# A three-layer chain on one core: the first layer's front by seven products instead of eight, and all attention ahead of it

## The chip, the cores and the metric

The kernel runs on one core of a Trainium2 chip. Its engines run side by side, each through its own instructions in order: TensorE (PE; its weight loads are listed as PEld), VectorE (DVE), ScalarE (ACT), GpSimd (POOL) and SyncE (SP), whose queue issues most DMA transfers. The metric is the device time of one launch in microseconds (us).

## The reference

Three stages follow one another on 2304 tokens (4 batches of 576) of 512 features:

```python
scores = scale * np.matmul(q, k.transpose(0, 1, 3, 2))   # 8 heads of 64
ret = scores * Dmat                                       # causal decay gamma_h ** (i - j)
x = np.matmul(ret, v)                                     # tokens x 512
# layer A, d_ff 1536
xn = x / np.sqrt(np.mean(x * x, -1, keepdims=True) + 1e-06) * rms_g
g = xn @ w_gate
x2 = (g * (1.0 / (1.0 + np.exp(-g))) * (xn @ w_val)) @ w_out
# layer B, d_ff 2048
h = x2 @ w_in
out = np.where(h >= 1, h, np.where(h <= -1, 0.0, (h + 1) ** 2 / 4)) @ w_out2
```

The weights arrive as 64-bit floats, in pairs of 32-bit words.

## The kernel before, in words

**Threefold products.** The products run in the type fp32r. Each fp32 operand is split into a high part rounded to it and the low rest (`split`: a cast on ScalarE, a subtraction on VectorE), and each product is issued three times (`three`): high by high, low by high, high by low, into one PSUM bank.

**Attention** goes by chunks of 128 tokens (the fifth of a batch has 64). `scores` multiplies K and Q of the 8 heads; VectorE applies the decay table; GpSimd scales Q and K (`qs`, `ks`). `values` adds what the batch's running state gives (`state`), the chunk's own part, and the chunk's addition to the state, which VectorE adds in SBUF. ScalarE copies the result out of PSUM and squares it; GpSimd sums the squares over features (`sq`, `sum`). Batches come one after the other. The first 7 chunks run ahead of layer A, the other 13 between its products (`att_step` in `step_a`).

**Layer A** takes the tokens in five blocks of 512, 512, 384, 512 and 384, and for each the 12 slices of 128 hidden features: 60 steps. A step has two front products (gate and value), each of 4 x 3 matmuls, then sigmoid on ScalarE and two multiplications and a split on VectorE, and 4 x 3 matmuls back for the previous step's slice, summed over the 12 slices in four banks. In the first block each step's weights are converted from 64-bit words (`convert`: Prelu on ScalarE, shift and merge on VectorE), stored as fp32 in DRAM (`wa32`), and split; later blocks load them back and split them again.

**Layer B** takes blocks of 768 tokens. Its front is already done by Strassen's algorithm in Winograd's form: token halves and feature halves make a 2 x 2 product out of 7 products (`product`) instead of 8, of sums of the weights (`prepare_in`) and of x (`sums_x`). Its weights are converted, summed and split while layer A runs (`prepare`, in the steps that `PREPARE` lists), stored in DRAM split, and loaded for each of the 24 steps. The back products of a step fill the gaps between the front products of the next.

**Order.** Nothing is issued as it is written. Class `Plan` records every operation (so the trace gives one line, L135, for all), and `issue` sorts them by a list schedule with a cost per operation and due times counted backward from TensorE's order. It keeps each engine's own queue in the order it finds; TensorE's rank is the program's order, with matmuls that are ready taken ahead by up to 100 ns.

## Time and profile before

| | before |
|---|---|
| three runs | 919.15, 920.0, 921.18 us; median 920.0 |
| profiled execution | span 920.9 us, 0.9 over the median, inside the three runs' spread |
| TensorE busy | 904.3 us (98%), 5098 matmuls |
| VectorE, ScalarE, GpSimd busy | 576.2, 482.3, 70.3 us |
| mean granted TensorE clock | 0.998 of full speed |
| DMA | 209.94 MB, mean 228 GB/s |

In the profile's rows a group is named by engine, operation, what it writes <- what it reads, with the tile names of the program, partitions x elements, and its count. `fr` are the two PSUM banks of the front products, `acc` and `at` the banks behind; `xall` holds the split x, `wt` the split weights, `h` the split hidden values; `att` are the attention buffers, used again in layer B for temporaries. Of an fp32 (not fp32r) matmul the trace shows two instructions. "Idle before" is the engine's idle time ahead of the group, with what ended it.

### The profile page before, as it was taken

What the parts mean: (1) busy time and instruction counts of PE and PEld (TensorE: products, weight loads), DVE (VectorE), ACT (ScalarE), POOL (GpSimd) and SP (SyncE); (2) the same over time, 40 slices, a digit from 0 to 9 for tenths busy, and PEclk for the clock granted to TensorE, in tenths of its full rate; (3) what the DMA queues carried; (4) which work ended last, traced back from release to release, by engine and by line L of the source; (5) the groups of instructions that cost most, each with busy time, mean ns of one, the idle gap of its engine ahead of it and who ended that gap; (6) DMA issues with size and microseconds to landing.
All of it is one profiled execution on the core that took longest, in us unless ns stands there. A gap on an engine that the chain in (4) does not pass through costs nothing.

```text
span 920.9 us, 13342 instructions
## 1 busy us (share of the span) xinstructions
PE 904.3 (98%) x5098; PEld 797.7 (87%) x5098; DVE 576.2 (63%) x929; ACT 482.3 (52%) x858; POOL 70.3 (8%) x80
## 2 busy tenths in 40 slices
PE   8799999999999999999999999999999999999998
PEld 7578888888889998888899998989888998989896
DVE  3978888888988888855658645434734345434343
ACT  3446665555765576533545454445654455644443
POOL 4620001310014001100000000000000000000000
PEclk9999999999999999999999999999999999999999
DMA  9679976988769984642254386646765454755432
GB/s 364 229 261 314 308 278 235 331 331 325 283 240 378 387 291 150 234 150 94 103 202 153 104 329 243 216 160 216 251 222 194 169 191 170 266 165 213 159 137 69
DMA packets 51647, 209.94 MB, mean 228 GB/s; under 512 B 5632, under 2 KB 11392, under 8 KB 47488
## 3 DMA queue, kind: packets, MB, share of 16 engines
q1 hardware_dynamic: 45392, 199.51, 61.2%
q10 hardware_dynamic: 6192, 9.59, 2.8%
q8 instruction: 40, 0.66, 0.3%
q14 instruction: 23, 0.19, 0.1%
HBM read 167.14 MB, written 41.94 MB: 227 GB/s over the span
## 4 chain that ended last, share of the span: by engine, by line
PE 92%; DVE 4%; DMA 2%; ACT 2%; issue 1%; ACTq 0%
PE fr L135 50%; PE acc L135 31%; PE at L135 11%; DMA out_dram<-o 1%; DMA att<-in_att_dram 1%; DVE xraw L135 1%; DVE xall L135 0%; DVE t L135 0%; DMA gk_sb<-in_gk_dram 0%; DVE w L135 0%; DVE wt L135 0%; ACT att L135 0%; DVE state L135 0%; DVE wsum L135 0%; DVE wpair L135 0%
## 5 line engine op out<-in xcount | busy, mean ns | idle before, releaser
L135 PE MATMUL fr<-xall,wt 128*128 128x384 f32 (+1 forms) x2424 | 512.1, 356 | 3.6 <-DVE xall L135 1.3
L135 PEld LDWEIGHTS fr<-xall,wt 128*128 128x128 f32 x2424 | 436.8, 188 | 53.5 <-DVE xall L135 2.4
L135 PE MATMUL acc<-h,wt 128*128 128x512 f32 (+1 forms) x708 | 158.1, 370 | 0.1
L135 PE MATMUL acc<-wprep,h 128*128 128x512 f32 x576 | 155.7, 394 | 0.5 <-ACT h L135 0.5
L135 PEld LDWEIGHTS acc<-h,wt 128*128 128x128 f32 x708 | 128.4, 188 | 18.2 <-ACT o L135 0.6
L135 DVE TENSOR_TENSOR wt<-w,wt 128x512 fp32r<-128x512 f32 (+1 forms) x118 | 114.4, 985 | 17.7 <-ACT wt L135 17.3
L135 PEld LDWEIGHTS acc<-wprep,h 128*128 128x128 f32 x576 | 106.6, 188 | 15.8 <-ACT h L135 0.9
L135 ACT CAST wt<-w 128x512 fp32r<-128x512 f32 (+1 forms) x118 | 96.7, 835 | 42.1 <-PE acc L135 23.6
L135 DVE TENSOR_TENSOR t<-fr,t 128x512 f32<-128x512 f32 (+1 forms) x120 | 76.3, 636 | 58.0 <-PE fr L135 29.5
L135 ACT ACTIVATE att<-att 128x384 f32<-128x384 f32 x156 | 79.2, 523 | 30.1 <-DVE att L135 18.2
L135 ACT CAST h<-t 128x512 fp32r<-128x512 f32 (+1 forms) x60 | 34.6, 577 | 79.3 <-DVE t L135 79.3
L135 DVE TENSOR_TENSOR att<-fr,att 128x384 f32<-128x384 f32 x48 | 26.6, 555 | 70.6 <-ACT att L135 69.6
L135 PE MATMUL at<-wprep,h 128*128 128x512 f32 x288 | 70.3, 392 | 0.0
L135 DVE TENSOR_TENSOR h<-att,h 128x384 fp32r<-128x384 f32 x96 | 52.8, 554 | 23.7 <-ACT h L135 23.1
L135 ACT ACTIVATE t<-fr 128x512 f32<-128x512 f32 (+1 forms) x60 | 33.3, 554 | 59.0 <-PE fr L135 58.7
L135 PEld LDWEIGHTS at<-wprep,h 128*128 128x128 f32 x288 | 53.7, 188 | 10.4
L135 ACT COPY att<-fr 128x384 f32<-128x384 f32 x48 | 23.0, 479 | 75.7 <-PE fr L135 70.2
L135 ACT CAST h<-att 128x384 fp32r<-128x384 f32 x96 | 48.7, 512 | 21.2 <-DVE att L135 20.0
L135 DVE SCALAR_TENSOR_TENSOR att<-att,att 128x384 f32<-128x384 f32 x48 | 26.8, 558 | 42.3 <-ACT att L135 42.3
L135 DVE TENSOR_TENSOR h<-t,h 128x512 fp32r<-128x512 f32 (+1 forms) x60 | 38.0, 634 | 14.2 <-ACT h L135 13.9
L135 DVE SCALAR_TENSOR_TENSOR att<-att,fr 128x384 f32<-128x384 f32 x24 | 13.3, 553 | 36.8 <-ACT att L135 36.8
L135 DVE TENSOR_TENSOR xall<-xraw,xall 128x512 fp32r<-128x512 f32 (+2 forms) x32 | 25.9, 828 | 2.8 <-ACT xall L135 2.4
(144 smaller groups left out, 672.5 us busy)
## 6 DMA issues: line engine op xcount, KB each, us to landing
w<-wa SPq DMA_DIRECT2D x48, 768.0 KB, 4.5
wprep<-wod SPq DMA_DIRECT2D x48, 512.0 KB, 4.0
wt<-wfd SPq DMA_DIRECT2D x24, 1024.0 KB, 5.2
wt<-wfd SPq DMA_DIRECT2D x24, 768.0 KB, 4.5
...
```

The lines of the kernel that those rows point to most:

```text
L135: call = lambda: getattr(real, method)(*args, **kwargs)
```

## The change

Layer A's front is also done by the seven products, over three blocks of 768 tokens: 36 steps, in each of which the 2 x 2 product gives gate and value of 128 hidden features for both token halves. The product back is split in 512 and 256 columns, four banks and two half-used ones; its 8 pieces fill the gaps between the front products. In the first block each step's weights are converted, summed and split (`prepare_a`) for the step after, and stored in DRAM in the split form (`store_a`: 1.8 MB, and the out weights as fp32, 0.26 MB); later blocks load them (`load_a`) and split only the out weights. `wts` are two buffers.

All attention stands ahead of A. Two batches alternate chunk by chunk; the state sums up in PSUM and ScalarE copies it out. The x of blocks two and three goes through two halves of `xout` to DRAM (`x1d`) on SP and comes back a block later. The gate uses ScalarE's Silu in the place of sigmoid and a product. Of layer B's 8 weight slices 5 are prepared in the later blocks of A, three (`LATE`) in B's first block. `later_than` lets the plan place some operations only behind a given one. Layer B's products are as before.

The order shows it at three places. First TensorE in layer A: before, a step of 12 gate and 12 value matmuls, the 12 of the previous step back, and the scores of a chunk in between (`at_0_145<-att`):

```order
L135 MATMUL fr_138<-xall_113,wt_151 128x512 x12
L135 MATMUL fr_139<-xall_113,wt_151 128x512 x12
L135 MATMUL acc_0_142<-h_154,wt_152 128x512 x3
L135 MATMUL acc_0_143<-h_154,wt_152 128x512 x3
L135 MATMUL acc_0_140<-h_154,wt_152 128x512 x3
L135 MATMUL acc_0_141<-h_154,wt_152 128x512 x3
L135 MATMUL fr_138<-xall_113,wt_152 128x512
L135 MATMUL at_0_145<-att_126 128x128 x3
L135 MATMUL fr_138<-xall_113,wt_152 128x512 x11
```

After, a whole step, 42 matmuls of 384 columns in `fr`, with pieces of 256 (`at`) and 512 (`acc`) of the previous step's slice between them (the last piece and two front products follow):

```order
L136 MATMUL fr_99<-xall,wt_64 128x384 x6
L136 MATMUL fr_100<-xall,wt_64 128x384 x6
L136 MATMUL fr_99<-xall,wt_64 128x384 x6
L136 MATMUL at_93<-h_67,wo 128x256 x6
L136 MATMUL fr_100<-xall,wt_64 128x384 x6
L136 MATMUL at_94<-h_67,wo 128x256 x6
L136 MATMUL fr_99<-xall,wt_64 128x384 x6
L136 MATMUL acc_95<-h_67,wo 128x512 x3
L136 MATMUL acc_96<-h_67,wo 128x512 x3
L136 MATMUL acc_97<-h_67,wo 128x512 x3
L136 MATMUL fr_99<-xall,wt_64 128x384
L136 MATMUL fr_100<-xall,wt_64 128x384 x6
```

The scores are gone from the steps, and the fill stands by pieces in between. Where A begins, the last chunks' values (state, then the chunk's own part) and the first front products mix on TensorE:

```order
L136 MATMUL at_93<-prep,state 128x128 x4
L136 MATMUL at_93<-prep,att_84 64x128 x8
L136 MATMUL acc_98<-att_83 64x64 x4
L136 MATMUL fr_99<-xall,wt_64 128x384 x3
L136 MATMUL at_94<-prep,state 128x128 x4
L136 MATMUL at_94<-prep,att_86 64x128 x8
L136 MATMUL fr_99<-xall,wt_64 128x384 x3
L136 MATMUL fr_100<-xall,wt_64 128x384 x4
L136 MATMUL at_93<-prep,state 128x64 x4
```

Ahead of these rows stand all the other chunks; before, 13 of 20 came later. Last, VectorE in the first block. Before, a step's gate (`t`, `h`) and the work on a next step's weights (`w`, `wt`):

```order
L135 TENSOR_TENSOR t_0_129<-fr_138,t_0_129 128x512
L135 TENSOR_TENSOR wt_151<-w_149,wt_151 128x512
L135 TENSOR_TENSOR t_0_131<-fr_139,t_0_129 128x512
L135 SCALAR_TENSOR_TENSOR w_150<-wpair_115,w_150 128x512
L135 TENSOR_TENSOR h_153<-t_0_131,h_153 128x512
L135 TENSOR_SCALAR w_149<-w_149 128x512
L135 SCALAR_TENSOR_TENSOR w_149<-wsum_116,w_149 128x512
L135 TENSOR_TENSOR wt_152<-w_150,wt_152 128x512
L135 TENSOR_SCALAR w_149<-w_149 128x512 x2
L135 SCALAR_TENSOR_TENSOR w_149<-stage_121,w_149 128x512
L135 TENSOR_TENSOR t_1_130<-fr_138,t_1_130 128x512
```

After, part of a step; the gate's seven operations (`att`, `h`, here six of them) stand between sums (`wsum`), low parts (`wt`, `wo`), and behind these rows two shifts, two merges and more sums follow up to the next step's first add:

```order
L136 TENSOR_TENSOR att_86<-fr_100,att_86 128x384
L136 TENSOR_TENSOR wsum<-wpair,wsum 128x256
L136 TENSOR_TENSOR wt_65<-wpair,wt_65 128x2x256
L136 TENSOR_TENSOR att_83<-fr_99,att_87 128x384
L136 TENSOR_TENSOR att_84<-att_86,att_85 128x384
L136 TENSOR_TENSOR wt_65<-wsum,wt_65 128x4x256
L136 TENSOR_TENSOR wo<-w32o_73,wo 128x512
L136 TENSOR_TENSOR h_67<-att_84,h_67 128x384
L136 TENSOR_TENSOR att_87<-fr_99,att_88 128x384
L136 TENSOR_TENSOR h_67<-att_83,h_67 128x384
L136 TENSOR_TENSOR wt_65<-wpair,wt_65 128x256
```

The adds out of PSUM (`fr`) are now three per step, one more than the products of gate and value, and low parts of seven weight operands stand between them instead of three.

The diff, cut to its core:

```diff
-BLOCKS = [512, 512, 384, 512, 384]
-STARTS = [sum(BLOCKS[:i]) for i in range(len(BLOCKS))]
...
+SB = 2 * TB
...
+W7 = 14 * 2 * P
...
-PREPARE = [(), (1, 3, 5, 7), (5, 7), (1, 3, 5, 7), (0, 1, 2, 3, 5, 6)]
+ATT = 6
+LATE = (3, 5, 7)
+EARLY = tuple(p for p in range(NPB) if p not in LATE)
...
+        if self.floor is not None and engine != "tensor":
+            before.add(self.floor)
...
-        table = {ACTF.Sigmoid: 1, ACTF.Abs_reciprocal_sqrt: 2}.get(kwargs.get("func"), 0)
+        table = {ACTF.Silu: 1, ACTF.Abs_reciprocal_sqrt: 2}.get(kwargs.get("func"), 0)
...
+    wfa = dram.tile([NA, P, W7], F32, name="wfa")
+    woa = dram.tile([NA, P, DM], F32, name="woa")
...
+    x1d = dram.tile([P, KD, NT], F32, name="x1d")
...
+        nc.vector.tensor_scalar(out=w, in0=w, scalar1=3, scalar2=None, op0=ALU.logical_shift_left)
...
+    def prepare_a(s):
+        prepare_front(wts[s % 2], None)
+        w = w32o[s % 2]
+        convert(w)
+        w = w.bitcast(F32)
+        split(w, wos[s % 4][:, :DM], wos[s % 4][:, DM:])
+
+    def prepare_back(p, ready):
+        convert(wpair_w)
+        for f, (w, r) in enumerate(zip(cut(wpair, DM), ready)):
+            split(w, r[:, :DM], r[:, DM:])
+            nc.sync.dma_start(out=wod[p, f], in_=r.bitcast(F32))
+
+    def store_a(s):
+        nc.sync.dma_start(out=wfa[s], in_=wts[s % 2].bitcast(F32))
+        nc.sync.dma_start(out=woa[s], in_=w32o[s % 2].bitcast(F32))
...
+    def load_a(s):
+        f = s % NA
+        load_front(wts[s % 2], wfa[f])
+        w = w32o[s % 2].bitcast(F32)
+        nc.sync.dma_start(out=w, in_=woa[f])
+        split(w, wos[s % 4][:, :DM], wos[s % 4][:, DM:])
...
+    chunks = [(b, c) for pair in ((0, 1), (2, 3)) for c in range(NCH) for b in pair]
...
+    staged = itertools.cycle(cut(xout[:, :2 * DM], DM))
...
+        x, new = banks[f"at{i % 2}"], banks[f"fr{b % 2}"]
...
-                nc.tensor.matmul(new[r, u], lhsT=ks[:, 2 * u + h], rhs=v[:, 2 * u + h], start=True, stop=True)
+                nc.tensor.matmul(
+                    new[r, u], lhsT=ks[:, 2 * u + h], rhs=v[:, 2 * u + h], start=c == 0 and u == 0, stop=c == NFULL - 1,
+                    skip_group_check=True,
+                )
...
-                if c:
-                    nc.vector.tensor_add(out=state[r, :, r], in0=state[r, :, r], in1=new[r])
-                else:
-                    nc.scalar.copy(out=state[r, :, r], in_=new[r])
+                nc.scalar.copy(out=st[r, :, r], in_=new[r])
...
+        sq = xout[:, 2 * DM:2 * DM + NPAIR * n].rearrange("p (u n) -> p u n", n=n)
+        edges = [g0] + [e for e in (TB, SB) if g0 < e < g0 + n] + [g0 + n]
+        for lo, hi in zip(edges, edges[1:]):
+            src = x[:, :, lo - g0:hi - g0]
+            if lo < SB:
+                nc.scalar.copy(out=x_j[lo // TB][:, :, lo % TB:lo % TB + hi - lo], in_=src)
+            else:
+                xs = next(staged)[:, :NPAIR * (hi - lo)].rearrange("p (u n) -> p u n", u=NPAIR)
+                nc.scalar.copy(out=xs, in_=src)
+                nc.sync.dma_start(out=x1d[:, :, lo:hi], in_=xs)
+        nc.scalar.activation(out=sq, in_=x[:, :, :n], func=ACTF.Square)
+        nc.gpsimd.tensor_add(out=sq[:, :2], in0=sq[:, :2], in1=sq[:, 2:])
+        nc.gpsimd.tensor_add(out=ss[:, g0:g0 + n], in0=sq[:, 0], in1=sq[:, 1])
...
-    def step_a(s):
-        _, t, f = steps[s]
-        T = BLOCKS[t]
...
-        nc.scalar.activation(out=u[:, :T], in_=g[:, :T], func=ACTF.Sigmoid)
-        nc.vector.tensor_mul(out=u[:, :T], in0=g[:, :T], in1=u[:, :T])
...
+    def back_a(s):
+
+        b, f = divmod(s, NA)
+        w, h = wos[s % 4], hs[s % 3]
+        big = [banks[f"acc{d}"] for d in range(KD)]
+        small = [banks[f"at{d // 2}"][:, d % 2 * 256:d % 2 * 256 + 256] for d in range(KD)]
+
+        def part(d, wide):
+            ps, q = (big[d], slice(0, 512)) if wide else (small[d], slice(512, SB))
+            c = slice(d * P, (d + 1) * P)
+            lo = slice(SB + q.start, SB + q.stop)
+            three(
+                ps, w[:, :DM][:, c], w[:, DM:][:, c], h[:, q], h[:, lo], f == 0 and (wide or d % 2 == 0), f == NA - 1,
+                skip_group_check=True,
+            )
+            if f == NA - 1 and (wide or d % 2):
+                o = next(o_next)
...
+    def gated(c):
+        g = temp("g", 2)
+        nc.scalar.activation(out=g, in_=c, func=ACTF.Silu)
+        return g
+
+    def keep(r, h, j):
+        split(r, h[:, j * TB:(j + 1) * TB], h[:, SB + j * TB:SB + (j + 1) * TB])
+
+    def step_a(s):
+        b, f = divmod(s, NA)
+        if s + 1 < NA:
+            with nc.later_than(marks[-4] if s == 0 else None):
+                prepare_a(s + 1)
+        units = back_a(s - 1) if s else []
+
+        def fill(n):
+            for _ in range(min(n, len(units))):
+                units.pop(0)()
+
+        after = split_x if f == NA - 1 else (lambda j: None)
+        w, h = wts[s % 2], hs[s % 3]
+        d, x = front_banks(s)
+        product(w, 0, d, True, False)
+        after(0)
+        if s < NA:
+            with nc.later_than(len(nc.ops) - 1):
+                store_a(s)
+        p1 = temp("p1", 1)
+        nc.scalar.copy(out=p1, in_=d)
+        product(w, 1, x, True, True)
+        after(1)
+        c = temp("c", 2)
+        nc.vector.tensor_add(out=c, in0=x, in1=p1)
+        g0 = gated(c)
+        product(w, 2, d, False, False)
+        after(2)
+        u2 = temp("u2", 2)
+        nc.scalar.copy(out=u2, in_=d)
+        fill(2)
+        product(w, 3, x, True, False)
+        after(3)
+        fill(2)
+        if s == 0:
+            rms(2, ("at0", "at1"))
+        product(w, 4, d, False, False)
+        after(4)
+        u3 = temp("u3", 2)
+        nc.scalar.copy(out=u3, in_=d)
+        nc.vector.tensor_add(out=u3, in0=x, in1=u3)
+        fill(2)
+        product(w, 5, x, False, True)
+        after(5)
+        nc.vector.tensor_add(out=u2, in0=x, in1=u2)
+        g1 = gated(u2)
+        r = temp("r", 2)
+        nc.vector.tensor_mul(out=r, in0=g1, in1=u3)
+        keep(r, h, 1)
+        fill(1)
+        product(w, 6, d, False, True)
+        after(6)
+        r = temp("r", 2)
+        nc.vector.tensor_mul(out=r, in0=d, in1=g0)
+        keep(r, h, 0)
+        fill(1)
+        if f == 0:
+            if b + 1 < NSB:
+                load_x(x1d, b + 1)
+                norm(b + 1)
+            else:
+                load_x(x2d, 0)
+            sums_x()
+        if s >= NA and s % 2:
+            limit[0] = len(slots)
+            with nc.later_than(len(nc.ops) - 1):
+                prepare_b()
+        if s + 2 >= NA:
+            if s + 2 < NSB * NA:
+                load_a(s + 2)
+            elif s + 2 == NSB * NA:
+                load_wf(0)
+                load_wo(0, 0)
+            else:
+                load_wf(1)
...
+        if q + 2 in LATE:
+            prepare_front(wts[q % 2], wfd[q + 2])
...
+    marks = []
+    for i in range(len(chunks) + 1):
+        if i < len(chunks):
+            scores(i, next(tags))
+        marks.append(len(nc.ops) - 1)
         if i:
...
+            values(i - 1)
+        for k in range(NSB - 1):
+            if ready[k] == i - 1:
+                rms(k, next(tags))
+                if k == 0:
+                    norm(0)
+                    sums_x(True)
+        if i == 4:
+            with nc.later_than(marks[2]):
+                prepare_a(0)
+    for s in range(NSB * NA):
         step_a(s)
```

## Rows read from the trace of the kernel before

**Rows 1.** The page's first part: busy us of each engine, share, instructions.
```profile
PE 904.3 (98%) x5098; PEld 797.7 (87%) x5098; DVE 576.2 (63%) x929; ACT 482.3 (52%) x858; POOL 70.3 (8%) x80
```

**Rows 2.** Stretches: start:end, length; PE, PEld, DVE, ACT, POOL busy (instructions); clock; DMA share, GB/s.
```profile
0.00:37.70 37.70, 29.76 (x362) 26.09 (x362) 20.37 (x35) 15.65 (x29) 19.05 (x25) 0.95 0.87 319
...
60.00:140.00 80.00, 79.97 (x367) 65.34 (x366) 69.57 (x116) 49.82 (x79) 3.65 (x5) 1.00 0.87 301
...
200.00:300.00 100.00, 99.92 (x612) 86.15 (x611) 84.20 (x136) 59.23 (x97) 12.96 (x16) 1.00 0.81 299
...
537.20:920.90 383.70, 378.43 (x1878) 338.76 (x1876) 162.78 (x292) 191.13 (x396) 0.00 (x0) 1.00 0.57 196
```

**Rows 3.** Chain of waits in order of time: start us, us, what.
```profile
54.29 3.01 PE fr L135 x12
...
100.68 5.44 PE fr L135 x24
...
473.59 4.16 PE fr L135 x24
```

**Rows 4.** TensorE in order of time, 164 to 176 us: start us, us.
```profile
174.31 1.05 PE L135 MATMUL at<-qs,state 128*128 128x128 f32 x8
```

**Rows 5.** GpSimd's groups by shape: busy us, mean ns of one, idle before.
```profile
L135 POOL TENSOR_TENSOR sq<-sq 128x256 f32<-128x256 f32 x14 | 14.0, 998 | 12.7 <-ACT sq L135 12.7
...
L135 POOL TENSOR_TENSOR qs<-att,gq_sb 128x512 f32<-128x512 f32 x8 | 11.5, 1435 | 76.5 <-PE at L135 65.5 <-issue 4.5 <-PE acc L135 3.6
...
L135 POOL TENSOR_TENSOR ks<-att,gk_sb 128x512 f32<-128x512 f32 x10 | 11.4, 1140 | 29.5 <-DMA att<-in_att_dram 25.2 <-PE at L135 4.3
...
L135 POOL TENSOR_TENSOR sum<-sq 128x128 f32<-128x128 f32 x14 | 8.3, 593 | 0.9
```

**Rows 6.** The opening in order of time, GpSimd: start us, us, what.
```profile
10.89 1.04 POOL L135 TENSOR_TENSOR ks<-att,gk_sb 128x512 f32<-128x512 f32 x1 [2.70 <-DMA att<-in_att_dram]
...
18.94 0.73 POOL L135 TENSOR_TENSOR sq<-sq 128x256 f32<-128x256 f32 x1
...
19.75 0.46 POOL L135 TENSOR_TENSOR sum<-sq 128x128 f32<-128x128 f32 x1
...
33.91 1.29 POOL L135 TENSOR_TENSOR qs<-att,gq_sb 128x512 f32<-128x512 f32 x1 [4.49 <-issue]
```

**Rows 7.** VectorE's groups by shape.
```profile
L135 DVE TENSOR_TENSOR wt<-w,wt 128x512 fp32r<-128x512 f32 x59 | 41.9, 711 | 6.7 <-ACT wt L135 6.5
...
L135 DVE TENSOR_TENSOR att<-fr,att 128x384 f32<-128x384 f32 x48 | 26.6, 555 | 70.6 <-ACT att L135 69.6 <-PE fr L135 1.0
...
L135 DVE SCALAR_TENSOR_TENSOR w<-stage,w 128x512 uint32<-128x512 uint32 x26 | 17.6, 685 | 0.1
...
L135 DVE TENSOR_SCALAR w<-w 128x512 uint32<-128x512 uint32 x36 | 16.1, 458 | 7.7 <-ACT w L135 7.3
...
L135 DVE TENSOR_TENSOR wprep<-wsum,wprep 128x1024 fp32r<-128x1024 f32 x8 | 11.1, 1393 | 0.5 <-ACT wprep L135 0.4
...
L135 DVE TENSOR_TENSOR wsum<-wpair 128x256 f32<-128x256 f32 x16 | 7.2, 468 | 0.1
...
L135 DVE SCALAR_TENSOR_TENSOR xraw<-xraw,gk_sb,y 128x384 f32<-128x384 f32 x8 | 4.9, 612 | 0.0
...
L135 DVE TENSOR_TENSOR wprep<-wpair,wprep 128x256 fp32r<-128x256 f32 x8 | 3.3, 415 | 0.0
...
L135 DVE TENSOR_TENSOR xall<-xraw,xall 128x768 fp32r<-128x768 f32 x12 | 11.5, 954 | 2.6 <-ACT xall L135 2.4
```

**Rows 8.** ScalarE's groups by shape.
```profile
L135 ACT ACT_TABLE_LOAD x11 | 14.1, 1283 | 3.7 <-issue 3.5
...
L135 ACT ACTIVATE t<-fr 128x384 f32<-128x384 f32 x24 | 11.8, 492 | 18.8 <-PE fr L135 18.6
```

**Rows 9.** DMA issues: queue, count, KB each, median us to landing.
```profile
x2d<-o ACTq DMA_DIRECT2D x12, 256.0 KB, 5.0
...
wsum<-in_tail_dram SPq DMA_DIRECT2D x1, 128.0 KB, 10.8
```

More of the change, by code (lines that the diff above doesn't have):

```diff
@@ L263, in moe_chain_kernel @@
-    stages = [stage_p.tile([P, DM, 2], U32, tag="stage", name="st") for _ in range(STAGE)]
-    more = [*stages, *(a.rearrange("p (n w) -> p n w", w=2) for a in (wpair_w, wsum_w))]
-    stage_of = [more[i % len(more)] if 9 <= i < 3 * NA - 2 else stages[i % STAGE] for i in range(len(slots))]
+    one = ctx.enter_context(tc.tile_pool(name="one", bufs=1))
+    psum = ctx.enter_context(tc.tile_pool(name="psum", bufs=1, space=PSUM))
+    dram = ctx.enter_context(tc.tile_pool(name="dram", bufs=1, space=DRAM))
@@ new lines, in moe_chain_kernel @@
+    stages = [one.tile([P, DM, 2], U32, name=f"stage{i}")[:, :, :] for i in range(STAGE)]
+    ss = sb("ss", NT)
+    o_sb = sb("o", 3 * DM)
+    gk_sb = sb("gk_sb", NFULL * H + KD)
+    eps = sb("eps", 1)
+    ones = sb("ones", P)
+    atts = [sb(f"att{i}", 8 * CH) for i in range(ATT)]
+    prep = sb("prep", 8 * DM)
+    dg = sb("dg", H * CH + NPAIR * (S - CH))
+    states = sb("state", 2 * NPAIR * P)
+    xout = sb("xout", 3 * DM)
+    banks = {n: psum.tile([P, 512], F32, name=n)[:, :] for n in ("at0", "at1", "acc0", "acc1", "acc2", "acc3", "fr0", "fr1")}
@@ new lines, in moe_chain_kernel, with split @@
+    gq_sb = dg[:, H * CH:]
+    state = [a.rearrange("p (u n) -> p u n", u=NPAIR) for a in cut(states, NPAIR * P)]
+    x_j = [a.rearrange("p (k n) -> p k n", k=KD) for a in cut(xraw, KD * TB)]
+    def split(src, hi, lo):
+        nc.scalar.copy(out=hi, in_=src)
+        nc.vector.tensor_sub(out=lo, in0=src, in1=hi.bitcast(F32))
+    slots = [wa[f, :, j * DM:(j + 1) * DM] for f in range(NA) for j in range(3)]
+    slots += [wb[p, k, j] for p in EARLY + LATE for k in range(2) for j in range(2)]
@@ L267, in load_slot @@
+    stage_t, loaded, taken, limit = {}, [0], [0], [3 * NA]
     def load_slot():
         i = loaded[0]
-        if i < len(slots):
-            st = stage_of[i]
-            assert all(st is not b for b in stage_t.values())
+        if i < limit[0]:
+            st = stages[i % STAGE]
             nc.sync.dma_start(out=st.rearrange("p a b -> p (a b)"), in_=slots[i].bitcast(U32))
@@ L359, in moe_chain_kernel @@
-    chunks = [(b, c) for b in range(B) for c in range(NCH)]
-    first, ahead = need(0), need(0) + AHEAD
-    buffers = [att_p.tile([P, 8 * CH], F32, tag="att") for _ in range(ATT)]
-    xraws = [xraw_p.tile([P, KD, 512], F32, tag="xraw", name="xraw") for _ in range(2)]
-    flat = xraws[1].rearrange("p k n -> p (k n)")
-    early = [*buffers, wpair, wsum, flat[:, :1024], flat[:, 1024:], o_sb[:, :]]
-    place = [early[i] for i in range(8)] + [early[i % 5] for i in range(8, 2 * ahead)]
-    place += [buffers[i % ATT] for i in range(2 * ahead, 2 * len(chunks))]
@@ new lines, in load_front @@
+    def load_front(w, src):
+        for a, b in ((0, 3), (3, 7)):
+            nc.sync.dma_start(out=w[:, a * 4 * P:b * 4 * P].bitcast(F32), in_=src[:, a * 4 * P:b * 4 * P])
+    def load_a(s):
[5 more added lines that the diff above has]
+    chunks = [(b, c) for pair in ((0, 1), (2, 3)) for c in range(NCH) for b in pair]
+    place = [*atts, wpair, wsum] + [atts[i % ATT] for i in range(2 * len(chunks))]
@@ L677, in product, with front_banks @@
             )
+    def front_banks(step):
+        d, x = banks["fr0"], banks["fr1"]
+        if step % 2:
+            d, x = x, d
+        return d[:, :TB], x[:, :TB]
+    def back_a(s):
[13 more added lines that the diff above has]
+                o = next(o_next)
+                nc.scalar.copy(out=o, in_=banks[f"acc{d}" if wide else f"at{d // 2}"])
+                if wide:
+                    nc.scalar.dma_start(out=x2d[:, d, b * SB:b * SB + 512], in_=o)
+                else:
+                    o = o.rearrange("p (d n) -> p d n", d=2)
+                    nc.scalar.dma_start(out=x2d[:, d - 1:d + 1, b * SB + 512:(b + 1) * SB], in_=o)
+        return [lambda d=d, wide=wide: part(d, wide) for wide in (False, True) for d in range(KD)]
```

492 lines of the change are left out of this document (148 added, 344 removed).

## The prediction

> **What bounds the kernel now.** I read the busy shares first, then the stretches, then the chain of waits, then the groups of instructions. The shares say that TensorE works 904.3 of the 920.9 us [rows 1]. By stretches, TensorE is full from 60 us on (79.97 of 80, 99.92 of 100), while VectorE is already 84 to 87% busy there; only the opening has holes: 29.76 us of work in the first 37.7 [rows 2]. The chain shows what a full TensorE costs: 24 products of 512 columns take 5.44 us and 24 of 384 take 4.16 [rows 3], so 226.7 and 173.3 ns each, 53.4 ns per 128 columns and some 13 ns besides. So a change pays here by products taken away, and loses wherever TensorE has to wait; today it waits for 16.6 us in all.
>
> **The sum by TensorE.** Layer A now: 60 steps, 36 of 512 tokens and 24 of 384; each has 24 products in front and 12 behind. That is 36 x 36 x 226.7 ns + 24 x 36 x 173.3 ns = 443.5 us. After: 36 steps (3 blocks of 768 tokens, 12 steps each) of 7 x 6 = 42 products of 384 columns (7.28 us), and behind 12 of 512 and 12 of 256. No row has a rounded-fp32 product of 256 columns. By the line through 512 and 384 it is 120 ns; the nearest row with a fresh 128 x 128 weight load each time is the state product, 8 in 1.05 us, 131 ns [rows 4]. A loss of weight-load cover could not show below 120, so I take 120 and keep +432 x 11 ns = 5 us for the upper end. A step is then 7.28 + 2.72 + 1.44 = 11.44 us, 36 are 411.9 us: TensorE loses 31.6 us of work. That is all the change has to gain; the rest is where it makes TensorE wait. I add the time by four stages.
>
> At this split a rule of the Trainium skill speaks against the change. The 384-column pair passes every 173.3 ns [rows 3], so its weight load costs at most the 13 ns that columns don't explain. The Trainium skill (TensorE: Matmul & The Clock Gate, "LDWEIGHTS" and "The mechanism") puts a 128-column load at some 107 ns and says that it overlaps running matmuls only on other row groups. By that rule the 256-column products would cost about 107 ns more each, 46 us in all; the trace contradicts it at 384 columns, and I leave it a small chance.
>
> **Stage 1, the opening: 86 us.** Now 7 of the 20 attention chunks run ahead and 13 between the products of A; the first unbroken dozen of A's products starts at 54.29 us [rows 3]. After, all 20 run ahead. TensorE isn't the slow one there: a full chunk's GpSimd work is 1.435 + 1.140 + 0.998 + 0.593 = 4.17 us at mean prices [rows 5]. All of GpSimd's work is 70.3 us [rows 1], and the change leaves it nearly as it is (two pieces fewer at block edges): 70. The last 4 us (the last chunks' sums) hold nothing up. The first of it can start at 10.89 us, when K and V of the first chunk have landed [rows 6]. Never idle, it would let A start at 10.9 + 66 = 77 us. As idle as in the opening now, where at most 19.05 us of its work lie in the 26.8 us from 10.9 to 37.7 (71%) [rows 2], it would be 104. Two things that held it then are gone: each chunk waited for its own batch's state, and now two batches alternate, and the state sums up in PSUM. I take 88% busy, 9 us of holes: 86, nearer the low end; bounds 77 and 104. VectorE's share lies beside it: 32 score multiplies of 512 and 8 of 256 (26 us by the nearest rows, 0.711 and 0.415), the first block's norm, sums and lows (14.5), two norm factors (6) and the first weights (8.4), 55 us or 64% of the stage [rows 7]; where that cover fails, A starts late within the same 104.
>
> **Stage 2, the first sweep of A: 160 us.** TensorE needs 12 x 7.28 + 11 x 4.16 = 133 us (step 0 has nothing to fill in). VectorE needs more. Preparing one step's weights is now [rows 7]: a shift of 1024 (no row; between 0.46 and 0.92, I take 0.73) and one of 512 (0.458), three merges (2.06), four sums of 256 (1.87), lows of 512, 1024 and 256 (0.711 + 1.393 + 0.415) and of the out weights (0.711): 8.35 us. The gate is 7 operations of 384 columns at 555 ns: 3.89. Together 12.2 us in a step of 11.44. Ten whole preparations fall into the sweep and 5.3 us of another; with 12 gates, the next block's norm (4 x about 1.0, from 612 ns at 384 columns), four sums and seven lows of 768 (11 x 0.954) and 2 us of the last norm this makes 152 us. Even with no hole it ends 2 us after that: 154. At the 87% of the first sweep now [rows 2] (where TensorE was the bound, so a floor) it would be 175. VectorE has weights to prepare whenever the gate doesn't call, so I take 95%: 160. The waits show as TensorE waiting for VectorE's adds out of PSUM: behind a late add stand the next products into that bank and, in TensorE's order, everything else.
>
> The DMA of this stage is 1.5 MB of raw weights, 1.8 + 0.26 MB stored per step, 3.6 MB in 13.3 us, 270 GB/s; now 301 GB/s run beside a full TensorE [rows 2], so I give it nothing. On SP's queue the stores stand in front of the raw loads of the next step; if a store is late, the loads, ScalarE's conversion and VectorE's shift are late behind it, which is the 175.
>
> **Stage 3, sweeps two and three: 279 us.** 24 x 11.44 = 274.6. VectorE falls to 3.89 + 0.71 us per step, plus a B weight every second step. Loads are 2.05 MB per step and up to 1.2 MB for B, 284 GB/s, under the 301 that hid. The shortest cover in a step is between product 4 and 5, where copy and add (under 0.5 by the row for sigmoid [rows 8], and 0.56, and their hand-overs) stand against two or three wide fills (1.4 to 2 us). I add 4 us for all of these and for the block ends, from 0 to 10.
>
> **Stage 4, layer B: 388 us.** Now 383.7 [rows 2]. The step of A left over costs 4.16 instead of 0.7 there: +3.5. Three of eight B weights are now prepared inside the first block: 6.5 us at most beside 6.1 of gate (11 operations of 555 ns) in a step of 16, VectorE 42% busy on average: 1 us, up to 5.
>
> **At no cost.** ScalarE's own Silu takes the place of sigmoid and a multiply; nearest row 492 ns for sigmoid of 384 columns [rows 8]; ScalarE is 59% busy in the sweep [rows 2], and that hides it (without cover: 72 x 0.5 us). The table loads fall from 11 to 4, 9 us [rows 8], hidden by the same slack already, so no gain.
>
> 86 + 160 + 279 + 388 = 913 us of profiled time. The profile's 920.9 is 0.9 above the median of 920.0, so the forecast is **912 us**.
>
> **Rivals.** (a) VectorE's excess in the first sweep hides behind TensorE (its holes elsewhere take it): stage 2 is 135, the total 887. For: TensorE was full at 87% VectorE. Against: only two weight buffers, so no step's preparation can start before the step two ahead has freed its buffer. (b) Slower: the staging store of the opening. 14 pieces of x go through two halves of one buffer to DRAM, on SP behind the loads of chunks, and ScalarE's third copy waits for the first store to land; behind that copy, in ScalarE's order, wait the squares and the state copies, and for them GpSimd and TensorE. A store of this size lands in 5.0 us, but a transfer of the present opening took 10.8 [rows 9]. Two chunks then need 10.8 + 1 us, 5.9 per chunk instead of 4.2: 14 x 1.7 = 24 us more, 936. It decides from about 9 us of landing on. (c) VectorE and GpSimd keep each other waiting. The undisturbed prices 1.29, 1.04, 0.73 and 0.46 [rows 6] stand against the means of [rows 5]; over the opening (12 + 16 + 16 + 16, and halves of them for the tails) they sum to 56 us. VectorE's operations with both inputs in SBUF are some 25 us there (norm 4, sums and lows 10.5, norm factors 4, first weights 7). If each holds GpSimd up in full, it works 81 instead of 70: 11 us, total 923. The Trainium skill (SBUF — State Buffer, "Who interferes with whom") states just this, an exclusive lock for the whole instruction; GpSimd's 70 us, 14 over the undisturbed sum, bear out a part of it. (d) Weight loads uncovered at 256 columns, bounded by a whole 384-column pair in place of the product: 432 x 53 ns = 23 us, 935. That the change doesn't do its sevenths is excluded by the order of TensorE's instructions.
>
> **Numbers.** Forecast 0.60, its own range 898 to 926 (stage 1 from 79 to 94, stage 2 from 154 to 168, not both ends at once); (a) 0.12; (b) 0.13; (c) 0.11; (d) 0.04. Of the forecast's case I put three quarters more than 0.2% under 920.0 (this is about what a measurement here can tell from no change), a tenth within; with (a), and a fifth of (c), this makes 0.60 faster. Same: 0.06 and four tenths of (c), 0.10. Slower: the rest, 0.30. The range 893 to 932 leaves out most of (a) and half of (b) and (d).
>
> **What would show it.** Right: the first unbroken products of A at 80 to 92 us with GpSimd the busiest engine before; in the next 160 us VectorE over 93% busy and TensorE near 84%; then steps of 11.4 to 11.7 us; B near 388. Wrong: steps of the first sweep at 11.4 us (a); ScalarE's copies into the staging buffer waiting for its stores (b); GpSimd means above 1.5 and 1.2 us (c); 256-column products over 131 ns apart (d).

## The result and the profile after

The changed kernel takes 899.8 us (899.5 to 901.9), the one before 920.0: ratio 0.9781, 95% interval 0.9766 to 0.9795, 20.2 us less. The forecast was 912, 8 us less. By the stages of the prediction, in profiled time:

| stage | forecast | measured | difference |
|---|---|---|---|
| 1 opening | 86 | 94.5 | +8.5 |
| 2 first sweep of A | 160 (154 to 175) | 138.3 | -21.7 |
| 3 sweeps two and three | 279 | 280.2 | +1.2 |
| 4 layer B | 388 | 384.7 | -3.3 |
| span and what lies around it | 913 | 897.7 | -15.3 |

(The cuts are where step 12 of A starts, 232.81, and step 0 of B, 513.0; stage 1 is the attention's end at 98.0 less 3.5 us, for some twenty products of A that ran between its last chunks.)

The page's first part, as in [rows 1]: TensorE works 23.7 us less.

```profile
PE 880.6 (98%) x5316; PEld 805.7 (90%) x5316; DVE 557.5 (62%) x955; ACT 487.6 (54%) x957; POOL 72.0 (8%) x76
```

The stretches of the kernel after, as in [rows 2]:

```profile
41.70:45.00 3.30, 3.13 (x34) 2.77 (x36) 3.30 (x6) 2.42 (x6) 2.56 (x1) 0.62 0.49 196
...
94.50:232.81 138.31, 137.31 (x789) 128.31 (x788) 125.68 (x235) 94.45 (x173) 2.03 (x5) 1.00 0.86 316
...
174.57:232.81 58.24, 58.24 (x332) 54.80 (x331) 54.45 (x102) 39.88 (x73) 0.00 (x0) 1.00 0.88 326
...
279.30:513.00 233.70, 232.65 (x1323) 219.22 (x1322) 142.80 (x249) 114.64 (x220) 0.00 (x0) 1.00 0.83 303
513.00:897.70 384.70, 380.80 (x1897) 341.87 (x1895) 188.13 (x335) 208.08 (x427) 0.00 (x0) 1.00 0.59 205
```

In the whole first sweep TensorE is full (137.31 of 138.31) and VectorE 91%. The forecast had it the other way round: VectorE over 93%, TensorE near 84%.

The chain of waits (start us, us, what), as in [rows 3], shows a step of A: 18 products of 384 columns in 3.14 us (174 ns each), 6 of 256 in 0.71 (118 ns), and the next step 11.62 us later.

```profile
302.81 3.14 PE fr L136 x18
305.95 0.71 PE at L136 x6
...
314.43 3.14 PE fr L136 x18
```

The sum of a step, 11.44, was short by 0.17 us. The ten changes of width in a step are the likely place: `plain8` below, with four of them, is 0.06 over its own sum. Stage 3's terms hold, and rival (d) is out: 120 ns was taken for 256 columns, 118 measured. The rule of the Trainium skill (TensorE: Matmul & The Clock Gate, "LDWEIGHTS" and "The mechanism") that would add 107 ns to each of these disagrees with the 118 ns of the trace here.

Where the first sweep's price went wrong shows in VectorE's own rows, in order of time (start us, listed us):

```profile
163.01 0.55 DVE L136 TENSOR_TENSOR att<-att,att 128x384 f32<-128x384 f32 x1
163.48 1.22 DVE L136 TENSOR_TENSOR wt<-wsum,wt 128x1024 fp32r<-128x1024 f32 x1
164.62 0.68 DVE L136 TENSOR_TENSOR wo<-w32o,wo 128x512 fp32r<-128x512 f32 x1
165.22 0.55 DVE L136 TENSOR_TENSOR h<-att,h 128x384 fp32r<-128x384 f32 x1
...
167.29 0.95 DVE L136 TENSOR_TENSOR dg<-xraw 128x768 f32<-128x768 f32 x1
168.16 0.69 DVE L136 SCALAR_TENSOR_TENSOR w32o<-stage,w32o 128x512 uint32<-128x512 uint32 x1
...
170.38 0.56 DVE L136 TENSOR_TENSOR att<-fr,att 128x384 f32<-128x384 f32 x1 [0.93 <-ACT att L136]
...
174.93 0.55 DVE L136 TENSOR_TENSOR att<-att,att 128x384 f32<-128x384 f32 x1
```

Subtract the starts: 0.47, 1.14, 0.60 us, where 0.55, 1.22, 0.68 are listed. Each of the first four rows begins 0.08 us before the one above ends. From 163.01 to the same operation of the next step at 174.93 are 11.92 us; less the idle 0.93 and one sum of the next block (0.87 from 167.29), preparation and gate cost 10.1 us, where the forecast added up 12.2.

The opening is the other miss. GpSimd's groups, as in [rows 5], rose in part as rival (c) would have them (ks, `prep<-att,gk_sb`, from 1140 to 1309 ns; the sums, `xout` and `ss`, from 998 and 593 to 1077 and 759). The other scaling did not (qs, `prep<-att,dg`, from 1435 to 1419), and GpSimd works 72.0 us in all, not the 81 of (c):

```profile
L136 POOL TENSOR_TENSOR prep<-att,gk_sb 128x512 f32<-128x512 f32 x15 | 19.6, 1309 | 11.0 <-DMA att<-in_att_dram 10.2 <-PE at L136 0.7
L136 POOL TENSOR_TENSOR xout<-xout 128x256 f32<-128x256 f32 x16 | 17.2, 1077 | 6.6 <-ACT xout L136 6.5
L136 POOL TENSOR_TENSOR prep<-att,dg 128x512 f32<-128x512 f32 x11 | 15.6, 1419 | 3.1 <-PE at L136 2.5 <-DMA att<-in_att_dram 0.6
L136 POOL TENSOR_TENSOR ss<-xout 128x128 f32<-128x128 f32 x16 | 12.1, 759 | 0.8
```

But TensorE's longest hole (a stretch in which it stands idle), 3.22 us up to 41.67, waits for VectorE, whose queue holds the first weights ahead of the score multiplies (prep):

```profile
32.24 2.97 DVE L136 SCALAR_TENSOR_TENSOR wpair<-stage,wpair 128x512 uint32<-128x512 uint32 x2
35.14 2.36 DVE L136 TENSOR_TENSOR wsum<-wpair 128x256 f32<-128x256 f32 x2
...
39.15 1.26 DVE L136 TENSOR_TENSOR wsum<-wpair,wsum 128x256 f32<-128x256 f32 x1
...
40.94 1.93 DVE L136 TENSOR_TENSOR prep<-acc,dg 128x512 f32<-128x512 f32 x4
```

Two sums of 256 take 2.36 us there; alone, eight such additions take 2.70 (`bench` below). Behind the hole the granted clock is 0.62 (41.70:45.00 above).

The next longest hole, 2.67 us up to 66.77, has another maker. TensorE waits for ScalarE's copy out of PSUM, and ScalarE had stood 2.83 us before the square ahead of it, waiting for GpSimd's sums:

```profile
64.78 0.60 ACT L136 ACTIVATE xout<-at 128x512 f32<-128x512 f32 x1 [2.83 <-POOL ss L136]
...
66.77 2.05 PE L136 MATMUL at<-prep,state 128*128 128x128 f32 x8 [2.67 <-ACT xout L136]
```

### The profile page after: what moved, and what is told of

The parts are those of the page before. It is cut to its first block, busy times and chain, and to the rows that moved or that the text cites. A ratio compares the mean times of both kernels' runs of the same rounds, so it can differ in the third digit from the quotient of the medians.

```text
span 897.7 us, 14004 instructions
## 1 busy us (share of the span) xinstructions
PE 880.6 (98%) x5316; PEld 805.7 (90%) x5316; DVE 557.5 (62%) x955; ACT 487.6 (54%) x957; POOL 72.0 (8%) x76
## 4 chain that ended last, share of the span: by engine, by line
PE 90%; DVE 4%; ACT 1%; DMA 1%; issue 0%; POOL 0%; ACTq 0%; DVEq 0%; SPq 0%
PE fr L136 49%; PE acc L136 26%; PE at L136 15%; DVE xraw L136 1%; DVE prep L136 1%; DMA stage<-in_wb_dram 1%; DVE xall L136 1%; DVE wsum L136 0%; ACT att L136 0%; DVE wpair L136 0%; ACT h L136 0%; DVE o L136 0%; ACT wpair L136 0%; DVE att L136 0%; DVE w32o L136 0%
## 5 line engine op out<-in xcount | busy, mean ns | idle before, releaser
L136 PE MATMUL fr<-xall,wt 128*128 128x384 f32 x2520 | 500.3, 337 | 2.2 <-ACT att L136 1.9
L136 DVE TENSOR_TENSOR att<-fr,att 128x384 f32<-128x384 f32 x216 | 119.9, 556 | 165.0 <-ACT att L136 107.0
L136 ACT COPY att<-fr 128x384 f32<-128x384 f32 x180 | 86.0, 478 | 142.7 <-PE fr L136 139.7
L136 PE MATMUL acc<-wo,h 128*128 128x512 f32 x576 | 154.7, 393 | 0.4 <-ACT h L136 0.4
L136 PEld LDWEIGHTS acc<-wo,h 128*128 128x128 f32 x576 | 106.7, 188 | 16.3 <-ACT h L136 0.9
L136 PE MATMUL acc<-h,wo 128*128 128x512 f32 x432 | 117.1, 394 | 0.0
L136 PEld LDWEIGHTS acc<-h,wo 128*128 128x128 f32 x432 | 79.7, 187 | 10.3
L136 PE MATMUL at<-wo,h 128*128 128x512 f32 x288 | 70.1, 392 | 0.0
L136 PE MATMUL at<-h,wo 128*128 128x256 f32 x432 | 66.0, 282 | 0.0
L136 PEld LDWEIGHTS at<-h,wo 128*128 128x128 f32 x432 | 61.2, 188 | 1.2
```

The source lines that it names most:

```text
L136: call = lambda: getattr(real, method)(*args, **kwargs)
```

## Experiments

Ratios are to the kernel before, run beside each. After was not run again beside them; its level there is taken as 0.9781 times that of before, 900 to 901 us.

**1. A ladder on VectorE in the first sweep.** `lad1` repeats one low of each step's preparation, `lad3` two:

```
 def split(src, hi, lo, times=1):
     nc.scalar.copy(out=hi, in_=src)
-    nc.vector.tensor_sub(out=lo, in0=src, in1=hi.bitcast(F32))
+    for _ in range(times):
+        nc.vector.tensor_sub(out=lo, in0=src, in1=hi.bitcast(F32))
```

Expected of `lad1`:

> In each of the 11 weight preparations of the first sweep VectorE does the low part of the out weights (512 columns) twice; the result is the same. Theory Q (queued instructions overlap by some 85 ns, so VectorE needs 10.85 of the 11.63 us of a step and has 0.8 us to spare): the extra one costs about 0.62 us and is hidden, 900 to 902 us. Rival L (VectorE's listed durations are what it pays and it is already the bound of the sweep): 11 x 0.70 = 7.7 us more, 907.

Expected of `lad3`:

> As lad1, and the low part of the three sums (1024 columns) twice as well. Theory Q: 10.85 + 0.62 + 1.14 = 12.6 us of VectorE in a step of 11.63, the excess of 1.0 us is paid 11 times: 911, from 908 to 914. Rival L: 11 x 1.92 = 21 us more, 921. Rival S (VectorE's work ahead of the sweep makes room, no bound there at all): under 904.

Measured: lad1 904.1 (0.9823, 0.9801 to 0.9845), 3.3 us over after; lad3 912.5 (0.9907, 0.9893 to 0.9922), 11.7 over. L is out (7.7 and 21), and so is S. Q is right in lad3 and 2 us over its range in lad1. What Q missed is an idle moment that VectorE can't use. Shown are lad1's stretch of one step, of its last five steps, and what its TensorE waited for from 128 to 232 us (waited for: us, times, longest):

```profile
182.20:194.60 12.40, 11.98 (x69) 10.88 (x68) 11.63 (x24) 7.51 (x14) 0.00 (x0) 1.00 0.80 296
...
169.85:231.64 61.79, 59.67 (x331) 54.17 (x331) 57.97 (x111) 39.33 (x72) 0.00 (x0) 1.00 0.84 308
```
```profile
PE fr L136 <- DVE wt L136: 2.1, 5, 0.4
```

VectorE works 11.63 of 12.40; the other 0.77 it waits for ScalarE's copy of the first product, in order, with the weights behind it. TensorE waits five times for weights, in the last five steps; the first steps still run at 11.5 to 11.7 on a lead. In after, from 174.57 on, five steps hold 54.45 us of VectorE's work in 58.24 (above): 10.9 of work, the next block's sum included, and 0.75 idle in a step of 11.65. In lad1 0.60 us more of work (start to start) makes these steps 12.36, 0.71 longer, and the idle time stays. So after's sweep has no slack of VectorE's left in its last steps: both engines bind there. The 0.8 us that Q took for slack were these waits.

**2. VectorE's price by itself.** `bench` puts queues of eight additions in front of the kernel, alone and then beside 26 multiplies of GpSimd:

```
+for n in (256, 384, 768):
+    for i in range(8):
+        v.tensor_add(out=o[:, i % 2 * n:i % 2 * n + n], in0=a[:, :n], in1=a[:, SB:SB + n])
+...
+for i in range(26):
+    g.tensor_mul(out=z[:, 2 * DM:3 * DM], in0=z[:, :DM], in1=z[:, DM:2 * DM])
```

> After's kernel with a queue of VectorE additions in front of everything: eight each of 256, 384 and 768 columns with both inputs in SBUF, 384 with one input in PSUM, and 384 where each reads the one before; then the same again beside 26 GpSimd multiplies of 512 columns. Theory Q: without GpSimd start to start is 0.07 to 0.10 us under the listed duration where the additions are independent (384: 0.47 against 0.55), and about equal to it, or more, where each waits for the one before. Rival L: start to start equals the listed duration everywhere. For the opening: if VectorE and GpSimd keep each other waiting, the second set shows SBUF additions longer by half or more and those from PSUM less so; if not, the two sets agree within 10%.

VectorE in order of time (start, us for all of the row):

```profile
3.99 2.70 DVE L822 TENSOR_TENSOR prep<-prep 128x256 f32<-128x256 f32 x8
...
6.74 3.82 DVE L822 TENSOR_TENSOR prep<-prep 128x384 f32<-128x384 f32 x8
...
11.55 6.97 DVE L822 TENSOR_TENSOR prep<-prep 128x768 f32<-128x768 f32 x8
18.44 3.81 DVE L824 TENSOR_TENSOR prep<-acc,prep 128x384 f32<-128x384 f32 x8
...
22.75 4.12 DVE L826 TENSOR_TENSOR prep<-prep 128x384 f32<-128x384 f32 x7
...
27.33 27.44 DVE L822 TENSOR_TENSOR prep<-prep 128x256 f32<-128x256 f32 x24 [0.47 <-POOL xraw L829]
...
54.69 3.81 DVE L824 TENSOR_TENSOR prep<-acc,prep 128x384 f32<-128x384 f32 x8
```

Eight independent additions of 384 take 3.82 us, 0.47 from start to start, while the mean listed for one is 0.55; where each reads the one before, 4.12 for seven, 0.59. Q holds. In the second set the 24 additions that took 13.5 us (2.70, 3.82 and 6.97) take 27.4. GpSimd is at work in the first part of that only:

```profile
27.30:46.40 19.10, 0.00 (x0) 0.00 (x0) 19.04 (x14) 0.00 (x0) 18.03 (x13) 0.50 0.00 0
46.40:54.60 8.20, 0.00 (x0) 0.00 (x0) 8.17 (x11) 0.00 (x0) 0.00 (x0) 0.50 0.00 0
```

Thirteen multiplies and thirteen to fourteen additions in 19.1 us: they take turns, one multiply (1.04 alone) and one addition (0.34 to 0.47) every 1.46 us. Listed, an addition of 256 is 1.35 there and one of 384 1.59; the ten that follow without GpSimd, two of 384 and eight of 768, take 8.2 us, about what they take alone. With one input in PSUM (54.69, GpSimd at work from 54.85) nothing changes: 3.81. That is what the Trainium skill (SBUF — State Buffer, "Who interferes with whom") states of the port that the two share, and the trace agrees. In after's opening score multiplies, which read PSUM, keep 0.68 listed (mean of 32); merges (1.5), sums of 256 (1.2) and the norm's multiplies of 768 (up to 1.68, later 1.01) are longer.

**3. The sevenths alone undone.** `plain8` keeps all else and makes layer A's front of eight plain block products:

```
-product(w, 0, d, True, False)
-...
-product(w, 6, d, False, True)
+pair(0, 0, d); pair(1, 0, x)   # gate, value of the first 384 tokens
+pair(0, 1, d); pair(1, 1, x)   # of the second
```

> Layer A's front by eight plain block products of 12 (48 instructions of 384 columns a step) where Strassen's form has 42, all else as after: 768 tokens, attention in front, Silu, weights through DRAM. The weights and tokens need no sums; the gate is 4 VectorE operations of 384 where it was 7. If TensorE alone sets layer A: 36 x 6 x 173.3 ns = 37.4 us more, 937 (932 to 941). If the sevenths' extra sums on VectorE cost time somewhere: less than that, by as much as they cost; under 925 would say that a third of their gain was lost.

Measured 927.4 (1.0069, 1.0048 to 1.0091), about 27 over after, not 37. Its chain:

```profile
160.90 6.26 PE fr L136 x36
167.17 1.43 PE at L136 x12
168.60 2.08 PE fr L136 x12
...
173.44 6.26 PE fr L136 x36
```

A step takes 12.54, 0.92 more than after's 11.62 and not the 1.04 of six products, which fits its fewer changes of width (four in place of ten): 33 us in 36 steps. The span is 29.2 longer; the other 4 us are the opening's, which has fewer sums and lows for VectorE: its attention ends at 94.5, after's at 98.0. So the sevenths alone are worth more than the whole change, and the rest (768 tokens, the attention in front, the weights' way through DRAM), in this plain form, costs 6.5 us against before.

**4. Whose pace the opening has.** Work taken from GpSimd (`nosq` leaves out the sums of squares; `sqvec`, `sqred` give them to VectorE), from VectorE's first burst (`latew`, `earlyw`), or from its second (`rmslate`):

```
-nc.gpsimd.tensor_add(out=sq[:, :2], in0=sq[:, :2], in1=sq[:, 2:])            # nosq: both out
-nc.gpsimd.tensor_add(out=ss[:, g0:g0 + n], in0=sq[:, 0], in1=sq[:, 1])       # sqvec: nc.vector
+nc.vector.tensor_reduce(out=ss[:, g0:g0 + n], in_=sq.rearrange("p u n -> p n u"), axis=X, op=ALU.add)  # sqred
-if i == 4: later_than(marks[2])     # prepare_a(0); latew: i == 12, marks[10]; earlyw: i == 0, none
-rms(1, ...) in the attention        # rmslate: in step 0 of A
```

Expected of `sqred`:

> In the opening the sum of squares of each chunk is one VectorE reduction (512 to 128, one input in SBUF) where GpSimd had two additions. Theory K (in the opening GpSimd and those VectorE operations that have both inputs in SBUF run one at a time; undisturbed they are 56 + 23 = 79 us of the 84 from 10.7 to 94.5): GpSimd's part falls by 21 us, stage 1 from 94.5 to 84 to 88 (TensorE's own 69 us of attention from 10.7 on is the floor), 889 to 894. Rival V (VectorE's queue is the bound of the opening, the rest follows it): 20 x 0.6 = 12 us more on it, 905 or above.

Expected of `sqvec`:

> The two additions of each sum of squares moved from GpSimd to VectorE as they stand, both inputs in SBUF (0.34 and some 0.2 us each). Theory K: the common sum falls by 21 less 10 = 11 us: gain of a half to the whole of sqred's, 890 to 897. If what holds VectorE up is having more operations at all (V): slower than after, 905 or above.

Expected of `latew`:

> The first weights are prepared from the 12th chunk on, not the 4th: 6 us of VectorE leave the stretch 33 to 41, where the chain of waits runs through them, and come back in the second half. Theory K: the sum of the two engines is the same, 897 to 903. Rival Q1 (what delays the opening is only that these operations stand ahead of the first score multiplies): the hole of 4 us at 37 to 42 goes, 894 to 896.

Expected of `sqredlate`:

> sqred and latew together. Theory K: within 2 us of sqred. Rival Q1: 3 to 5 us under sqred.

Expected of `earlyw`:

> The first weights are prepared from the first chunk on (their buffers wpair and wsum no longer serve attention's chunks as well): 7 us of VectorE come from the stretch 30 to 46, where VectorE is full, to 10 to 30, where it works 6.75 of 20 us. Theory W (what holds TensorE up in the opening is VectorE's queue in two bursts, first weights at 30 to 46 and the first block's norm and sums at 57 to 90; relieving GpSimd by operations put on VectorE only swaps one price for the other): the hole of 3.2 us at 38 and the half clock behind it (1.3 us) go: 894 to 896. Rival D (the 1.6 MB of raw weights now stand before attention's loads in a DMA that is full until 30 us): 4 us lost there, 900 to 904.

Expected of `rmslate`:

> The norm factor of the second block (two multiplies of 768 and two copies of 512 and 256 on VectorE, 3 us) is worked out behind the attention. Theory W: VectorE is full at 60 to 83, but there the burst's end, not this, holds A up: 897 to 900. In the first sweep, where lad1 left some 0.6 us a step, it is hidden. Rival G (VectorE's queue is merely full, and the chunks are paced by GpSimd): no change, 899 to 901.

Expected of `earlyrms`:

> earlyw and rmslate together. Theory W: 890 to 895. Rival D: 898 to 903. Rival G: 900.

Expected of `nosq`:

> Leaves out the sums of squares: GpSimd's 40 additions are gone and nothing takes their place (the norm works with a constant); VectorE's operations are those of after. Measures what GpSimd's 31 us cost. Theory W with lock: VectorE's listed operations in 29 to 90 us hold some 14 us over their undisturbed prices; without the additions 6 of them go: 893 to 896. Rival G (GpSimd paces the opening): its work falls by 43%, the opening to TensorE's floor of 80 us, 886 to 888. If neither matters: 899 to 901.

Measured: sqred 905.1, sqvec 900.4, latew 908.2, sqredlate 905.7, earlyw 904.0, rmslate 903.9, earlyrms 903.2, nosq 900.5. None is clear of after on the faster side (the intervals are 2 to 3 us to either side).

- K and G are out: nosq works with 41 us of GpSimd in place of 72 and is no faster; it came out at the 899 to 901 expected if neither the wait for GpSimd nor its pace matters.
- Q1 is out: latew, which takes the first weights out of the way, is the slowest.
- V isn't shown either: sqred lies at its 905, but there a reduction cost 1.05 us, not 0.6, and sqvec's VectorE works 6.5 us more up to 105 us at no cost.
- W's rows are there, but its gains are not. D comes nearest, with 900 to 904 for earlyw and 898 to 903 for earlyrms. In earlyw a new hole waits for a load of attention's operands, as D has it, and the old one, still behind the first weights, is longer. Its attention ends 2 us sooner in the profiled execution; a third hole (3.3 us at 80, behind GpSimd's sums) and a later first step take that back:

```profile
20.91 2.43 PE L136 MATMUL acc<-att 64*128 64x128 f32 x32 [2.77 <-DMA att<-in_att_dram]
...
28.42 2.35 PE L136 MATMUL at<-prep,att 128*64 128x128 f32 x15 [3.99 <-DVE prep L136]
```

What the slow variants have in common is the clock. In nosq and in rmslate, after a hole:

```profile
30.00:45.00 15.00, 11.99 (x188) 10.44 (x184) 13.31 (x20) 9.34 (x20) 5.86 (x5) 1.00 0.84 292
45.00:60.00 15.00, 12.30 (x179) 11.15 (x180) 14.50 (x16) 7.58 (x15) 9.73 (x7) 0.89 0.79 268
60.00:75.00 15.00, 12.88 (x145) 10.31 (x142) 15.00 (x18) 7.29 (x14) 6.78 (x5) 0.87 0.68 225
```
```profile
37.30:40.50 3.20, 0.02 (x1) 0.00 (x0) 3.20 (x5) 1.18 (x2) 1.70 (x2) 0.90 1.01 342
...
45.00:60.00 15.00, 15.00 (x138) 12.53 (x138) 6.06 (x10) 5.29 (x12) 6.22 (x10) 0.60 0.67 210
```

rmslate has after's hole of 3.2 us, and then TensorE is busy all through 45 to 60 at a mean granted clock of 0.60: mostly the lower level, 1.2 GHz. Sixteen products of 64 columns take 1.12 us there (46.84) and 0.68 at full clock in after (49.46).

This differs from execution to execution of one program. rmslate's four took 900.1, 902.7, 905.2 and 907.3 us at mean granted clocks of 0.994, 0.992, 0.990 and 0.987; the profile shows the last. An estimate: take from each execution one less its mean clock, times its span. After's median is then 894.4, and all fourteen variants of this section and the next lie between 893 and 897, where as measured they lie between 893.8 and 908.2. So, by this estimate, most of what sets them apart is time at the lower clock in the opening, and a difference of 2 or 3 us between two of them is by itself no sign of a mechanism.

**5. The order of VectorE's queue.** The planner counts 0.68 us for a merge that takes 1.5 beside GpSimd. `price` tells it, for every VectorE operation with both inputs in SBUF; `sq2` adds a second buffer for the squares; the others combine these with each other and with section 4's:

```
-return each + 150 + n / 0.96
+return each + 150 + n / 0.96 + (self.lock if len(ins) == 2 and not psum else 0)   # 600 in the opening, then 0; price1000: 1000, with sq2's buffer
-sq = xout[:, 2 * DM:...]
+sq = (xout[:, 2 * DM:], w32o[1].bitcast(F32))[i % 2]                              # sq2 and its kin
```

Expected of `sq2`:

> A second buffer for the squares (w32o, unused until the attention's end), so that ScalarE's square of a chunk doesn't wait for GpSimd's sums of the chunk before. Theory H (the opening is TensorE's own 69 us from 10.7 on, 10 us of holes, and 4.6 us of half clock behind them; the holes have two makers, score multiplies behind a burst of VectorE's, and products behind ScalarE's copies and squares): the hole of 2.7 us at 64 and the half clock at 65 to 70 (1.7 us) go: 896 to 898. Rival N (the work of VectorE and GpSimd together decides, and holes only move): 899 to 901.

Expected of `sq2price`:

> sq2, and in the opening the planner counts 0.6 us more for every VectorE operation with both inputs in SBUF (what such an operation waits for GpSimd), so that it puts the score multiplies ahead of more of them. Theory H: the hole of 3.2 us at 38 and the half clock behind it go as well, 892 to 895. Rival N: 899 to 902.

Expected of `sq2pe`:

> sq2price and earlyw together. Theory H: earlyw's holes at 64, 70 and 80 (ScalarE's copies and squares and GpSimd's sums, 5.3 us) go, the one at 28 (4.0) shrinks: 891 to 895. Rival N: 899 to 903.

Expected of `sq2pv`:

> sq2price and sqvec together: VectorE makes the sums of squares. Theory H: as sq2price, or 1 to 2 us under it since less of VectorE's time is waiting for GpSimd: 890 to 895. Rival N: 898 to 901, VectorE being full in the burst.

Expected of `price`:

> The planner's 0.6 us alone, without the second square buffer. Theory H2 (sq2price gained 3 us by the order of VectorE's queue alone; ScalarE's wait for the sums is no maker of its own, as sq2 showed): 896 to 898, ratio to before 0.973 to 0.976. Rival (the two need each other): 899 to 901, ratio 0.978.

Expected of `price1000`:

> sq2price with 1.0 us in place of 0.6. If the price is only a way to put score multiplies first, more of it does no more and the first block's lows come later: 896 to 900. If attention still waits behind VectorE's queue, 893 to 895.

Measured: sq2 901.7, sq2price 896.8 (0.9745, 0.9727 to 0.9764), sq2pe 903.0, sq2pv 905.7, **price 893.8 (0.9707, 0.9694 to 0.9720)**, price1000 904.3. The price alone makes the best kernel, 27 us under before and 7 under after, 2 us better than H2's range. H fails in sq2, sq2pe and sq2pv, which gain nothing; sq2price lies between H and N. The second buffer gains nothing alone, and beside the price it costs 3 us. price1000 has that buffer too, so its neighbour is sq2price: 1.0 us in place of 0.6 costs 7.5, outside both of its ranges. VectorE's order in price, the score multiplies now ahead of the sums that follow the first two:

```profile
30.90 2.98 DVE L137 SCALAR_TENSOR_TENSOR wpair<-stage,wpair 128x512 uint32<-128x512 uint32 x2
33.80 2.36 DVE L137 TENSOR_TENSOR wsum<-wpair 128x256 f32<-128x256 f32 x2
36.09 1.93 DVE L137 TENSOR_TENSOR prep<-acc,dg 128x512 f32<-128x512 f32 x4
```

The stretches of after, then of price:

```profile
30.00:45.00 15.00, 10.94 (x150) 9.39 (x151) 15.00 (x19) 7.61 (x15) 12.16 (x10) 0.92 0.72 240
...
60.00:75.00 15.00, 11.88 (x148) 9.83 (x149) 15.00 (x16) 8.95 (x17) 14.92 (x13) 0.89 0.68 232
```
```profile
30.00:45.00 15.00, 13.47 (x207) 11.29 (x205) 13.21 (x18) 8.93 (x20) 13.18 (x15) 1.00 0.90 312
...
60.00:75.00 15.00, 13.54 (x192) 11.13 (x190) 11.01 (x13) 8.22 (x16) 13.33 (x13) 1.00 0.75 239
```

The 3.2 us hole is gone, and the clock is 1.00 in every stretch of price from 10 to 103 us. After's means of 0.91, 0.92, 0.97 and 0.89 over 20, 15, 15 and 15 us lose 5.1 us of full-clock work. From 10 to 90 us price is busy 2.7 us longer; together 7.8, of which 2 are given back behind the attention, by difference, where products wait for ScalarE (1.4 at 92, 1.0 at 100). The span is 5.8 shorter, so most of the gain is time at the lower clock that price does not have. It still has holes, the longest 1.5 us (59.27), and none of them is followed by a lower clock.

Open: why the second buffer, early weights or a price of 1.0 bring the lower clock back (mean clock 0.998 to 1.000 in price's executions, 0.996 to 0.998 in sq2price's, 0.989 to 0.994 in sq2pe's, 0.990 to 0.994 in price1000's). All of them change the order at many places at once, with nearly the same work. A place-by-place account wasn't made. So that price orders VectorE's queue otherwise and has no lower clock is shown; that this order, and no other effect of the new plan, is the cause is argued.

## Why the prediction was wrong

- **The step that failed is stage 2's price of VectorE.** "Together 12.2 us in a step of 11.44" is a sum of listed means, and made VectorE the bound of the sweep. Two things are wrong in it. Some means hold waits for GpSimd: of the eight 1024-column lows behind the 1.393 of [rows 7] two took 2.08 and 1.74 with GpSimd at work, the others 1.22 to 1.23, which is also the sweep's; at the sweep's own listed prices the sum is 11.7. And in a full queue listed durations overlap by 0.08 us each, twenty times a step (bench, and the starts at 163 us). Measured: 10.1. With it the step is TensorE's. Rival (a), which had 0.12 of the chance, has about this time, 135 against 138.3, but not this reason: it let an excess of VectorE hide behind TensorE, and there was none. The ladder shows how close it was: 0.60 us more a step, and VectorE was the bound of the last five steps.
- **The argument against (a)** (two weight buffers forbid working ahead) was beside the point: 10.1, or 10.9 with the next block's sum, and its waits fit into a step of 11.65 without a lead.
- **Stage 1 took 94.5, just over its own range (79 to 94), by another mechanism.** GpSimd, 70.0 us busy in it, isn't the pace: nosq works without 31 us of it and is no faster. What the trace has are TensorE's holes, the longest behind VectorE's order (3.2 us), one behind ScalarE and GpSimd's sums (2.7), one at the start behind a load (2.0), and the half clock after each (5.1 us of full-clock work in all, section 5). The prediction had no term for the clock. "Where that cover fails" named VectorE, but gave it no price. Rival (c) has a mechanism that is there (bench: turns), and its price is not: GpSimd worked 72.0 us, not 81. It lengthens the operations in VectorE's queue ahead of the score multiplies.
- **Stages 3 and 4** were right to 1.2 and 3.3 us; TensorE's sum (31.6 less) shrank to 23.7 of busy time, 6 us of it by the 0.17 a step. Rival (b) did not happen: the 14 stores landed in 2.6 to 7.6 us, and no copy of ScalarE waited for one.
- **The total is nearer than its parts.** 899.8 lies inside the stated range (893 to 932), and inside the forecast's own (898 to 926), by luck: stage 2 is 16 us under the lowest value that the range allowed it (154), and stage 1's 8.5 us on the other side take part of that back.
